# Masking the first batch on TensorE, and a new written order of the whole program

## The chip, the cores and the metric

The kernel runs on one core of one Trainium2 chip. The metric is the device time of one execution in microseconds (us); lower is better. The profile is that of one execution.

## The reference

Block-sparse attention is followed by a gated feed-forward block:

```
scores = (q @ k^T) / sqrt(64)                      # 4 batches, 8 heads, 768 tokens, 64 per head
scores = where(mask, scores, -1e9)                 # mask in blocks of 32 x 32 tokens: neighbours,
                                                   # first and last block, 3 sampled blocks a row
attn   = softmax(scores) @ v                       # -> x, 3072 tokens x 512
xn     = x / rms(x) * rms_g
out    = (silu(xn @ w_gate) * (xn @ w_val)) @ w_out   # 512 -> 1536 -> 512
```

The mask is the same for all batches and heads.

## The kernel before

**Tiling.** The 3072 tokens are twelve chunks of 256 (`ch` 0 to 11, three to a batch; `ic = ch % 3`). In a chunk attention goes over four pairs of heads (`pr`) and, in each pair, over three pieces of 256 keys (`j2`). One such piece is one score step `s0` to `s143`: `s12` to `s23` are chunk 1, `s24` to `s35` chunk 2, and so on. TensorE computes the transposed scores of two heads into two PSUM banks (L648), ScalarE takes the exponential of each bank (`x...`, L661), and after the three pieces TensorE multiplies by V (`av`, 24 matmuls, L678). V carries a column of ones, which gives the sum for the division (`on`, L690 and L692). Then come the squares (`sq`, L703 or L706), the power -1/2 on GpSimd (`rs`, L711), the scaling (`sc`, L717) and the transposition of x: on TensorE in chunks 0 and 1 (`xt`, L732, with the copies `xc`), by DMA from SyncE's queue later (`xd`).

The feed-forward part of a chunk `u` is six column pieces `g{u}_0` to `g{u}_5` of the two up projections (L835; 32 matmuls each), tanh (`th`, L842), two VectorE steps (`uu` L846, `h` L853), and the down projection `y{u}_t_part` (L868), whose result ScalarE copies out (`yo`).

**The mask** is applied in one of two ways. For the chunks that `PEM` names, TensorE adds a term to the scores in PSUM before the exponential. It comes from two small matrices, `KindG` and `NegQ`, and is 0 where a pair is allowed and -16384 where it is not (L653):

```python
def PEM(ch, pr):
    return ch == 0 or ch == 1 and pr < PM1        # PM1 = 0
...
start=True, stop=not PEM(ch, pr))
if PEM(ch, pr):
    nc.tensor.matmul(out=s_, lhsT=KindG[rows, 2 * j2 + jj, :],
        rhs=NegQ[rows, ic * CQ:(ic + 1) * CQ], start=False, stop=True)
```

All other chunks are multiplied after the exponential, on VectorE, by a mask of ones and zeros (`m{ch}_{pr}_{j2}`, L668). That mask, `Mk`, is made once, in nine tiles (`mt` on TensorE, `mk` on VectorE or ScalarE).

**Loads.** K, Q and V of batches 1 to 3 go through one staging buffer, `stage`. They are loaded in that order, each as two DMAs on GpSimd's queue (`l{b}_1_..` is K, `l{b}_0_..` Q, `l{b}_2_..` V), then cast: `c{b}_1_0` to `c{b}_1_5` for K, `c{b}_0_0` to `c{b}_0_5` for Q, `va{b}_0` to `va{b}_3` for V. The next of the three can load only when the last cast of the one before is done. The transposed K and Q of batches 1 to 3 come by DMA from SyncE's queue (`dt`). The weights use GpSimd's queue too: the up projections in six pieces (`wg`, `wv`), the down projection in two halves, `wo0_` and `wo1_` (L458). The parts 0 to 2 of `y0_0` need the first half, the parts 3 to 5 the second.

**Order.** The order of the instructions is written out: the string `ORDER` holds some 1500 steps, with the buffers (the digits after a colon) and, where two engines could do a step, the engine (`*DVE`, `*ACT`). Each engine executes its steps in this order, and each waits only for what it needs. The string was planned from assumed durations; the numbers in the `plan.add` calls are what such a planner uses, and at run time they do nothing. `FILL` sets the number of fillers `w0`, `w1`, ...: pairs of idle matmuls (L321).

GpSimd's steps from 40 us on are, in the string's order:

```
sta1_0 l1_0_0 l1_0_4 rs1 sta1_2 l1_2_0 wo1_ one1 l1_2_4 sta2_1 rs2 l2_1_0 l2_1_4
```

Of the kernel before, what the change touches and what calls it, by code (L numbers as in the profile page):

```python
# [27 lines left out]
x1_2_1_0 m1_0_1 sc0_0:0 sc0_1:1 e3_0_2*DVE w6:4 w7:4 xt0_0:10 xt0_1:4 s20:07 s21:36 x1_2_1_1 x1_2_2_0 x1_2_2_1
x1_3_0_0:3 xc0_0*DVE xc0_1*DVE m1_1_1 m1_1_2 m1_0_2 m1_2_1 m1_1_0 qk0 raw0 rawq1 xc0 w8:1 w9:2 g0_0a:12 g0_0
s22:45 s23:07 x1_3_0_1 th0_0:0 x1_3_1_0 x1_3_1_1 x1_3_2_0 x1_3_2_1 uu0_0:0 m1_2_2 h0_0:0 m1_3_0 m1_2_0  # L30
g0_1a:36 g0_1 s24:41 g0_2a:50 s25:72 g0_2 th0_1:1 x2_0_0_0:1 x2_0_0_1 x2_0_1_0 x2_0_1_1 th0_2:2 uu0_1:1 h0_1
m1_3_2 uu0_2:2 av1_0:4 s26:17 mt2_2:3 av1_2:2 s27:65 on1_0 m1_3_1 c1_1_0*DVE mk2_2*ACT x2_0_2_0 x2_0_2_1
x2_1_0_0:4 x2_1_0_1 c1_1_1*DVE c1_1_2*DVE c1_1_3*DVE c1_1_4*DVE c1_1_5*ACT h0_2 on1_2 g0_3a:31 s28:47 g0_3
av1_3:6 av1_1:5 w10:0 w11:0 s29:20 sta1_0 th0_3:0 x2_1_1_0 x2_1_1_1 x2_1_2_0 x2_1_2_1 on1_3 uu0_3:0 on1_1 h0_3
m2_0_2 m2_1_1 m2_1_2 sq1_0*ACT sq1_1*ACT l1_0_0 l1_0_4 rs1 s30:46 w12:7 g0_4a:37 g0_4 s31:25 s32:01 th0_4:1
x2_2_0_0:2 x2_2_0_1 x2_2_1_0 x2_2_1_1 x2_2_2_0 x2_2_2_1 uu0_4:1 sc1_0:2 sc1_1:3 h0_4 m2_0_1 m2_2_1 m2_2_0
m2_0_0 m2_2_2 c1_0_0*DVE c1_0_1*DVE c1_0_2*DVE c1_0_3*DVE w13:4 s33:43 w14:6 xt1_0:61 w15:2 xt1_1:5 s34:20
g0_5a:71 g0_5 xc1_0*ACT xc1_1*ACT x2_3_0_0:3 th0_5:2 x2_3_0_1 x2_3_1_0 x2_3_1_1 c1_0_4*ACT c1_0_5*ACT uu0_5:2
m2_3_1 h0_5 qk1 dt1_1_0 dt1_1_3 dt1_0_0 xc1 sta1_2 g1_0a:65 g1_0 g1_1a:43 g1_1 g1_2a:20 g1_2 s35:71 th1_0:0
th1_1:1 x2_3_2_0 x2_3_2_1 th1_2:2 uu1_0:0 uu1_1:1 m2_1_0 h1_0:1 h1_1 uu1_2:2 av2_2:6 mt0_0:4 s36:71 w16:5  # L40
s37:53 av2_0:2 mk0_0*ACT x3_0_0_0:0 x3_0_0_1 x3_0_1_0 x3_0_1_1 m2_3_0 h1_2 on2_0 on2_2 m2_3_2 l1_2_0 wo1_ one1
l1_2_4 s38:47 s39:15 s40:03 av2_1:2 av2_3:6 x3_0_2_0 x3_0_2_1 x3_1_0_0:2 x3_1_0_1 x3_1_1_0 x3_1_1_1 m3_0_1
on2_1 m3_1_0 on2_3 m3_0_2 m3_1_1 m3_0_0 va1_0*DVE va1_1*DVE va1_2*DVE va1_3*DVE s41:47 g1_3a:15 s42:20 s43:36
g1_3 x3_1_2_0 x3_1_2_1 x3_2_0_0:1 x3_2_0_1 x3_2_1_0 x3_2_1_1 th1_3:0 sq2_0 sq2_1 dt1_0_2 dt1_0_4 raw1 rawq2
sta2_1 rs2 l2_1_0 l2_1_4 y0_0_0:4 y0_0_1 s44:72 s45:03 y0_0_2 y0_0_3 y0_0_4 y0_0_5 av3_0:6 x3_2_2_0 x3_2_2_1
yo0_0:0 x3_3_0_0:4 x3_3_0_1 uu1_3:0 m3_1_2 h1_3 sc2_0:0 on3_0 m3_2_0 m3_2_2 m3_2_1 sc2_1:1 s46:17 s47:24
av3_1:5 s48:03 x3_3_1_0 x3_3_1_1 x3_3_2_0 x3_3_2_1 x4_0_0_0:3 x4_0_0_1 g1_4a:61 g1_4 s49:72 av3_2:4 s50:03
x4_0_1_0 th1_4:1 x4_0_1_1 x4_0_2_0 on3_1 m3_3_2 uu1_4:1 m3_3_1 on3_2 h1_4 m3_3_0 x4_0_2_1 g1_5a:57 g1_5 s51:26
s52:03 y0_1_0:4 y0_1_1 y0_1_2 av3_3:1 y0_1_3 th1_5:2 x4_1_0_0:0 x4_1_0_1 x4_1_1_0 c2_1_0*DVE c2_1_1*ACT
x4_1_1_1 c2_1_2*ACT uu1_5:2 on3_3 sq3_0 sq3_1 c2_1_3*DVE h1_5 c2_1_4*DVE c2_1_5*DVE m4_0_2 m4_0_1 xd2_0:2  # L50
xd2_1 qkfree0 xc2 qk2 dt2_1_0 dt2_1_3 sta2_0 l2_0_0 l2_0_4 rs3 y0_1_4 y0_1_5 s53:26 s54:05 g2_0a:31 g2_0
x4_1_2_0 x4_1_2_1 yo0_1:1 th2_0:0 x4_2_0_0:2 x4_2_0_1 uu2_0:0 h2_0:0 g2_1a:72 g2_1 s55:64 g2_2a:03 s56:51 g2_2
th2_1:1 x4_2_1_0 x4_2_1_1 x4_2_2_0 th2_2:2 x4_2_2_1 uu2_1:1 sc3_0:2 h2_1 sc3_1:3 m4_1_2 uu2_2:2 m4_0_0 h2_2
m4_1_1 m4_1_0 m4_2_0 m4_2_1 s57:67 y1_0_0:4 y1_0_1 y1_0_2 y1_0_3 y1_0_4 y1_0_5 s58:52 s59:10 x4_3_0_0:1
x4_3_0_1 yo1_0:2 x4_3_1_0 x4_3_1_1 x4_3_2_0 x4_3_2_1 g2_3a:67 g2_3 s60:43 g2_4a:52 s61:10 g2_4 th2_3:0
x5_0_0_0:4 x5_0_0_1 uu2_3:0 m4_2_2 m4_3_0 m4_3_1 x5_0_1_0 x5_0_1_1 th2_4:1 s62:46 av4_0:3 av4_2:1 av4_1:0
uu2_4:1 on4_0 on4_2 on4_1 m4_3_2 h2_3 h2_4 x5_0_2_0 c2_0_0*ACT x5_0_2_1 s63:45 g2_5a:36 g2_5 s64:10 av4_3:7
y1_1_0:2 y1_1_1 y1_1_2 y1_1_3 x5_1_0_0:3 c2_0_1*ACT c2_0_2*ACT c2_0_3*ACT th2_5:2 x5_1_0_1 on4_3 uu2_5:2
x5_1_1_0 h2_5 m5_0_0 c2_0_4*DVE c2_0_5*DVE x5_1_1_1 sq4_0 sq4_1 xd3_0:3 xd3_1 xc3 dt2_0_0 sta2_2 y1_1_4 y1_1_5
s65:45 g3_0a:71 s66:03 rs4 l2_2_0 l2_2_4 x5_1_2_0 x5_1_2_1 yo1_1:3 x5_2_0_0:2 x5_2_0_1 g3_0 s67:64 g3_1a:52  # L60
g3_1 s68:03 x5_2_1_0 x5_2_1_1 th3_0:0 th3_1:1 x5_2_2_0 x5_2_2_1 g3_2a:64 g3_2 s69:03 th3_2:2 x5_3_0_0:0
x5_3_0_1 va2_0*ACT m5_1_1 sc4_0:0 m5_1_0 uu3_0:0 uu3_1:1 h3_0:1 h3_1 m5_2_2 uu3_2:2 m5_0_2 g3_3a:75 g3_3
s70:12 y2_0_0:0 y2_0_1 y2_0_2 y2_0_3 y2_0_4 y2_0_5 s71:36 x5_3_1_0 th3_3:0 va2_1*ACT x5_3_1_1 va2_2*ACT
yo2_0:0 sc4_1:1 h3_2 m5_0_1 m5_3_1 uu3_3:0 m5_1_2 h3_3 x5_3_2_0 g3_4a:14 g3_4 s72:20 s73:73 y2_1_0:5 y2_1_1
y2_1_2 y2_1_3 x5_3_2_1 th3_4:1 x6_0_0_0:1 x6_0_0_1 uu3_4:1 h3_4 x6_0_1_0 x6_0_1_1 va2_3*ACT m5_2_1 m5_3_0
m5_2_0 m5_3_2 qkfree1 xd4_0:0 xd4_1 xc4 dt2_0_2 dt2_0_4 raw2 rawq3 sta3_1 y2_1_4 s74:62 s75:10 s76:74 av5_0:3
y2_1_5 x6_0_2_0 x6_0_2_1 yo2_1:1 x6_1_0_0:4 x6_1_0_1 x6_1_1_0 x6_1_1_1 av5_2:6 av5_3:2 av5_1:5 s77:10 on5_0
on5_2 m6_0_2 on5_3 on5_1 x6_1_2_0 x6_1_2_1 sq5_0 sq5_1 g3_5a:36 s78:72 g3_5 g4_0a:45 s79:10 g4_0 rs5 l3_1_0
l3_1_4 x6_2_0_0:2 x6_2_0_1 th3_5:2 x6_2_1_0 x6_2_1_1 th4_0:0 m6_1_2 m6_2_0 uu3_5:2 sc5_0:2 uu4_0:0 h4_0:0 h3_5
g4_1a:72 g4_1 g4_2a:13 g4_2 s80:04 th4_1:1 th4_2:2 x6_2_2_0 y3_0_0:5 y3_0_1 y3_0_2 y3_0_3 y3_0_4 y3_0_5 s81:60  # L70
x6_2_2_1 yo3_0:2 x6_3_0_0:0 x6_3_0_1 m6_2_1 uu4_1:1 uu4_2:0 h4_1 m6_2_2 sc5_1:3 h4_2 c3_1_0*DVE m6_1_1
c3_1_1*ACT g4_3a:74 g4_3 s82:12 s83:56 g4_4a:30 g4_4 th4_3:0 x6_3_1_0 m6_3_0 uu4_3:2 m6_1_0 c3_1_2*DVE h4_3
x6_3_1_1 x6_3_2_0 x6_3_2_1 g4_5a:17 g4_5 s84:25 s85:64 th4_4:1 c3_1_3*ACT uu4_4:1 m6_3_2 m6_0_1 c3_1_4*ACT
th4_5:2 x7_0_0_0:3 c3_1_5*ACT x7_0_0_1 x7_0_1_0 x7_0_1_1 uu4_5:0 h4_4 h4_5 m6_3_1 m6_0_0 xd5_0:1 xd5_1 xc5
sta3_0 y3_1_0:3 y3_1_1 y3_1_2 y3_1_3 y3_1_4 y3_1_5 s86:21 s87:50 s88:67 av6_2:4 yo3_1:3 x7_0_2_0 x7_0_2_1
# [88 lines left out]
def kernel(  # L164
# [20 lines left out]
    NP = H // 2  # L185
# [787 lines left out]
```

## Time and profile before

| | |
|---|---|
| median of six runs | 301.04 us (300.64 to 302.83) |
| the profiled execution | 300.78 us |
| its span on the core | 299.0 us |
| busy: PE, DVE, ACT | 286.1 us, 243.2 us, 232.2 us |
| VectorE mask multiplications (L668) | 132, 686 ns mean |
| TensorE mask matmuls (L653) | 48 |
| data moved by DMA | 39.76 MB |

PE is TensorE's matmuls, PEld its weight loads, DVE VectorE, ACT ScalarE, POOL GpSimd, SP SyncE. A row of the timeline is: start in us, length in us, engine, line, operation, what it writes and reads, how many instructions; in brackets, the idle time before it and what ended that. A row of a table of stretches is: from and to, length, then the busy us of PE, PEld, DVE, ACT and POOL with the count of instructions, the granted TensorE clock, the DMA share and GB/s. A row of loads ends with the KB of one and the us from issue to landing.

### The profile page before, as it was taken

What the parts mean: (1) busy time and instruction counts of PE and PEld (TensorE: products, weight loads), DVE (VectorE), ACT (ScalarE), POOL (GpSimd) and SP (SyncE); (2) the same over time, 40 slices, a digit from 0 to 9 for tenths busy, and PEclk for the clock granted to TensorE, in tenths of its full rate; (3) what the DMA queues carried; (4) which work ended last, traced back from release to release, by engine and by line L of the source; (5) the groups of instructions that cost most, each with busy time, mean ns of one, the idle gap of its engine ahead of it and who ended that gap; (6) DMA issues with size and microseconds to landing.
All of it is one profiled execution on the core that took longest, in us unless ns stands there. A gap on an engine that the chain in (4) does not pass through costs nothing.

```text
span 299.0 us, 10723 instructions
## 1 busy us (share of the span) xinstructions
PE 286.1 (96%) x4557; PEld 218.6 (73%) x4579; DVE 243.2 (81%) x501; ACT 232.2 (78%) x469; POOL 35.3 (12%) x56
## 2 busy tenths in 40 slices
PE   7999998995999999999999999999999999999995
PEld 4776987764776876787787678787778778678862
DVE  6679999985979979879988788999759889845840
ACT  7999989896698999978958899998398776242421
POOL 9531020303020030020100021000000000000000
PEclk9999999998899999999999999999999999999999
DMA  8999998993959944777543796502504104224003
GB/s 183 308 205 207 299 170 222 178 215 104 248 94 229 171 104 152 125 204 161 151 144 54 91 234 189 85 30 70 110 0 101 45 2 72 37 38 143 2 10 132
DMA packets 56692, 39.76 MB, mean 133 GB/s; under 512 B 42244, under 2 KB 50052, under 8 KB 56644
## 3 DMA queue, kind: packets, MB, share of 16 engines
q1 hardware_dynamic: 45268, 17.11, 31.6%
q0 software_dynamic: 10688, 21.50, 28.5%
q8 instruction: 36, 0.59, 0.8%
q10 hardware_dynamic: 688, 0.46, 0.5%
q14 instruction: 12, 0.10, 0.2%
HBM read 28.57 MB, written 6.29 MB: 117 GB/s over the span
## 4 chain that ended last, share of the span: by engine, by line
PE 81%; DVE 5%; DMA 5%; ACT 5%; issue 2%; POOL 1%; ACTq 0%
PE f L835 38%; PE f L868 20%; PE f L678 10%; PE f L648 9%; DMA stage<-in_v_dram 5%; ACT pt L661 4%; DVE pt L668 2%; PE f L321 2%; PE f L483 1%; DVE X L692 1%; DVE hp L853 1%; DVE uu L846 1%; PE f L732 1%; PE f L653 0%; ACT qb L269 0%
## 5 line engine op out<-in xcount | busy, mean ns | idle before, releaser
L661 ACT ACTIVATE pt<-f 128x512 bf16<-128x512 f32 x288 | 153.3, 639 | 11.7 <-PE f L648 11.4
L835 PE MATMUL f<-xn,wgv 64*128 64x256 bf16 x2304 | 137.5, 270 | 0.5 <-issue 0.5
L835 PEld LDWEIGHTS <-wgv 64*128 64x128 bf16 x2304 | 115.0, 94 | 13.3 <-issue 1.6
L668 DVE TENSOR_TENSOR pt<-pt,Mk 128x1024 bf16<-128x1024 bf16 x132 | 86.5, 686 | 4.2 <-ACT pt L661 4.1
L868 PE MATMUL f<-wo,hp 128*128 128x512 bf16 (+1 forms) x278 | 65.6, 370 | 2.8 <-DMA wo<-in_moe_w_out_dram 1.6
L842 ACT ACTIVATE th<-f 128x512 bf16<-128x512 f32 x72 | 44.0, 618 | 24.7 <-PE f L835 21.7
L846 DVE SCALAR_TENSOR_TENSOR uu<-th,f 128x512 bf16<-128x512 bf16 x72 | 48.7, 683 | 13.6 <-ACT th L842 13.5
L648 PE MATMUL f<-qkT 64*128 64x256 bf16 x576 | 52.9, 271 | 2.2 <-DVE uu L846 1.7
L853 DVE TENSOR_TENSOR hp<-uu,f 128x512 bf16<-128x512 bf16 x72 | 48.3, 684 | 2.2
L868 PEld LDWEIGHTS <-hp 128*128 128x128 bf16 x300 | 27.1, 98 | 31.3 <-issue 5.5
L678 PEld LDWEIGHTS <-pt 128*128 128x128 bf16 x1152 | 38.4, 97 | 8.0 <-issue 4.7
L678 PE MATMUL f<-va,pt 128*128 128x65 bf16 x1152 | 41.0, 194 | 0.9 <-DVE hp L853 0.6
L648 PEld LDWEIGHTS <-qkT 64*128 64x128 bf16 x576 | 26.4, 94 | 13.8 <-issue 10.1
L890 ACT ACTIVATE yo<-f 128x512 f32<-128x512 f32 (+1 forms) x24 | 14.1, 594 | 18.0 <-PE f L868 17.5
L711 POOL TENSOR_TENSOR rs<-ms,nhalf 128x2 f32<-128x2 f32 x12 | 9.1, 755 | 152.2 <-ACT junk L703 133.0
L717 DVE SCALAR_TENSOR_TENSOR x<-X,rs,gB 128x512 bf16<-128x512 f32 (+1 forms) x48 | 22.1, 514 | 3.4 <-POOL rs L711 3.4
L692 DVE TENSOR_TENSOR X<-f,rz 128x256 f32<-128x256 f32 x48 | 20.4, 425 | 1.7
L703 ACT ACTIVATE junk<-X 128x513 bf16<-128x513 f32 x22 | 14.1, 669 | 7.2 <-DVE X L692 7.2
L690 DVE RECIPROCAL rz<-f 128x4 f32<-128x4 f32 x48 | 8.5, 177 | 9.2 <-PE f L678 8.2
L321 PE MATMUL f<-idle 128*128 128x256 bf16 x48 | 8.8, 315 | 2.1 <-DVE idle L296 1.1
L275 POOL DMA_DIRECT2D stage<-in_q_dram x6 | 4.5, 762 | 41.8 <-ACT th L842 15.4
L269 DVE CAST va<-stage 128x768 bf16<-128x768 f32 x10 | 5.3, 554 | 4.5 <-DMA stage<-in_v_dram 4.4
(80 smaller groups left out, 111.4 us busy)
## 6 DMA issues: line engine op xcount, KB each, us to landing
stage<-in_v_dram POOLq DMA_DIRECT2D x8, 768.0 KB, 8.1
out_dram<-yo SPq DMA_DIRECT2D x23, 256.0 KB, 2.2
stage<-in_k_dram POOLq DMA_DIRECT2D x6, 768.0 KB, 7.0
stage<-in_q_dram POOLq DMA_DIRECT2D x6, 768.0 KB, 6.8
wgv<-in_moe_w_gate_dram POOLq DMA_DIRECT2D x3, 512.0 KB, 17.5
wgv<-in_moe_w_val_dram POOLq DMA_DIRECT2D x3, 512.0 KB, 19.3
wo<-in_moe_w_out_dram POOLq DMA_DIRECT2D x2, 768.0 KB, 17.2
xn<-x SPq DMA_TRANSPOSE x40, 3.6
```

Source lines behind the costliest of these rows:

```text
L321: nc.tensor.matmul(out=warm[:, 0:256], lhsT=idle[:, 0:P], rhs=idle, start=True, stop=True)
L648: nc.tensor.matmul(out=s_, lhsT=x[rows, 1, 2 * j2 + jj, pr, :], rhs=x[rows, 0, 2 * ic:2 * ic + 2, pr, :], start=True, stop=not PEM(ch, pr))
L661: nc.scalar.activation(out=pts[ch, pr][:, j2, e], in_=st[t][e], func=AF.Exp, scale=SCALE)
L668: nc.vector.tensor_tensor(out=pv, in0=pv, in1=m.unsqueeze(1).to_broadcast([P, 2, 2 * CQ]), op=ALU.mult)
L678: nc.tensor.matmul(out=o_[:, qt, e, 0:D + 1], lhsT=pt[:, jt // 2, e, jt % 2 * CQ + qt * P:jt % 2 * CQ + (qt + 1) * P], rhs=va[(ch // NIC) ...
L692: nc.vector.tensor_tensor(out=x1s[ch][:, :, 2 * pr * D:(2 * pr + 2) * D].rearrange("p t (h d) -> p t h d", h=2), in0=o4[:, :, :, 0:D], in1 ...
L717: nc.vector.scalar_tensor_tensor(out=x2[:, lo:lo + n], in0=x1s[ch][:, qt, 0:n], scalar=mss[ch][:, qt:qt + 1], in1=gB[:, 0:n], op0=ALU.mult ...
L835: nc.tensor.matmul(out=gst[u, fp, name][:, half * CQ:(half + 1) * CQ], lhsT=wgv[rows, dpart(i, c), f * P:(f + 1) * P], rhs=xns[u][rows, c, :],
L842: nc.scalar.activation(out=ths[u, fp], in_=gst[u, fp, "gp"], func=AF.Tanh, scale=0.5)
L846: nc.vector.scalar_tensor_tensor(out=uus[u, fp], in0=ths.pop((u, fp)), scalar=1.0, in1=gst.pop((u, fp, "gp")), op0=ALU.add, op1=ALU.mult)
L853: nc.vector.tensor_tensor(out=hps[u][:, 2 * fp:2 * fp + 2, :].rearrange("p f t -> p (f t)"), in0=uus.pop((u, fp)), in1=gst.pop((u, fp, "vp ...
L868: nc.tensor.matmul(out=yst[u, t, half][:, 0:n], lhsT=hps[u][:, f, t * P:(t + 1) * P], rhs=wo[:, f, cols], start=(f == 0), stop=(f == NF - 1))
```

## The change

1. `PEM` now names the first twelve pairs: all of chunks 0, 1 and 2, which is batch 0. Chunks 1 and 2 get the added matmuls and lose their 24 multiplications `m1_...` and `m2_...`.
2. Eleven fillers in place of 17.
3. Numbers of the planner: some landing and DMA times are set longer.
4. The string `ORDER` is planned anew. Names that stay move, change buffers, and 33 steps change between VectorE and ScalarE.

```diff
-    PM1 = 0
+    PMASK = 12
 
     def PEM(ch, pr):
-        return ch == 0 or ch == 1 and pr < PM1
-
-    FILL = 17
+        return ch * NP + pr < PMASK
+
+    FILL = 11
...
-    swdge("V4", lambda: load_v0(4), 2.4, [">V0"], -9, issue=0.75, extra=2.1)
+    swdge("V4", lambda: load_v0(4), 2.4, [">V0"], -9, issue=0.75, extra=2.8)
...
-                swdge(f"l{b}_{i}_{lo}", lambda b=b, i=i, lo=lo: load_part(b, i, lo, lo + 4), (3.6, 2.5, 2.5)[i],
+                swdge(f"l{b}_{i}_{lo}", lambda b=b, i=i, lo=lo: load_part(b, i, lo, lo + 4), 2.6,
...
-                     deps=[f"qk{b}"] + ([">" + prev] if prev else []) + [f"c{b}_{i}_{c}" for c in range(c0, c1)], dma=0.7 * (c1 - c0), prio=1)
+                     deps=[f"qk{b}"] + ([">" + prev] if prev else []) + [f"c{b}_{i}_{c}" for c in range(c0, c1)], dma=1.2 * (c1 - c0), prio=1)
```

On GpSimd's queue the new order is

```
sta1_0 l1_0_0 l1_0_4 rs1 sta1_2 l1_2_0 l1_2_4 wo1_ one1 sta2_1 l2_1_0 l2_1_4 rs2
```

so the second half of the down projection, which was issued between the two halves of batch 1's V, is issued behind both. Earlier on the same queue `rs0` now stands ahead of batch 1's K (`rs0 l1_1_0 l1_1_4 wo0_`, before `l1_1_0 l1_1_4 wo0_ rs0`).

The steps of ScalarE around batch 1's Q (the casts `c1_0_...`) are now

```
x2_2_2_1 th0_4 c1_0_0 x2_3_0_0 th0_5 xc1_0 x2_3_0_1 x2_3_1_0 x2_3_1_1 c1_0_5 x2_3_2_0 th1_0
```

and were

```
x2_2_2_1 xc1_0 xc1_1 x2_3_0_0 th0_5 x2_3_0_1 x2_3_1_0 x2_3_1_1 c1_0_4 c1_0_5 th1_0
```

TensorE's steps from the second chunk's feed-forward part on are now

```
w7 w8 s35 g1_0 g1_1 g1_2 av2_1 s36 s37 av2_0 mt0_0 s38 av2_3 s39 s40 av2_2 s41 g1_3a s42 g1_3
s43 s44 w9 w10 s45 y0_0_0 y0_0_1 y0_0_2 y0_0_3 y0_0_4 y0_0_5 s46 s47 s48 av3_0 av3_1 g1_4
```

and were

```
g1_0 g1_1 g1_2 s35 av2_2 mt0_0 s36 w16 s37 av2_0 s38 s39 s40 av2_1 av2_3 s41 g1_3a s42 s43 g1_3
y0_0_0 y0_0_1 s44 s45 y0_0_2 y0_0_3 y0_0_4 y0_0_5 av3_0 s46 s47 av3_1 s48 g1_4
```

## The prediction

> **What bounds the kernel now.** I read the page first.
>
> ```profile
> span 299.0 us, 10723 instructions
> PE 286.1 (96%) x4557; PEld 218.6 (73%) x4579; DVE 243.2 (81%) x501; ACT 232.2 (78%) x469; POOL 35.3 (12%) x56
> ...
> PE   7999998995999999999999999999999999999995
> ...
> DVE  6679999985979979879988788999759889845840
> ...
> PEclk9999999998899999999999999999999999999999
> ```
>
> TensorE is busy nearly everywhere. The exceptions are the start, the end, and slices 9 to 11 (60 to 82 us), where the granted clock dips too. Next I cut the span into stages, from 28.9 us, where the feed-forward matmuls begin.
>
> ```profile
> 28.90:66.20 37.30, 36.15 (x647) 29.81 (x648) 36.84 (x76) 34.47 (x70) 4.87 (x7) 1.00 1.04 216
> 66.20:81.00 14.80, 10.88 (x170) 8.38 (x172) 9.80 (x22) 9.63 (x22) 2.26 (x3) 0.88 0.80 184
> 81.00:264.00 183.00, 181.38 (x2911) 137.41 (x2928) 158.02 (x309) 150.39 (x307) 14.38 (x19) 1.00 0.51 109
> ```
>
> After 81 us PE is busy 181.38 of 183 us and the view of waits has 0.7 us of waits for it: that part is TensorE's own work, which the change leaves alone, so a VectorE relief is worth nothing there. From 28.9 to 66.2 us VectorE is full (36.84 of 37.30) with PE close behind. The hole is 66 to 81 us. The timeline of PE:
>
> ```profile
> 66.13 0.61 PE L868 MATMUL f<-wo,hp 128*128 128x512 bf16 x2
> 68.33 1.46 PE L868 MATMUL f<-wo,hp 128*128 128x512 bf16 x6 [1.59 <-DMA wo<-in_moe_w_out_dram]
> 69.62 0.89 PE L678 MATMUL f<-va,pt 128*128 128x65 bf16 x24
> 72.25 0.61 PE L648 MATMUL f<-qkT 64*128 64x256 bf16 x8 [1.74 <-DVE uu L846]
> 73.45 1.48 PE L678 MATMUL f<-va,pt 128*128 128x65 bf16 x24 [0.59 <-DVE hp L853]
> 74.86 0.61 PE L648 MATMUL f<-qkT 64*128 64x256 bf16 x4
> ```
>
> First y0_0_3 waits for wo1. Then s46 waits for a bank that uu1_3 frees. Then av3_1 takes 1.48 us where av3_0 took 0.89: the clock is at half from 73.07 to 76.48 us (granted 0.50 there). VectorE tells why uu1_3 is late:
>
> ```profile
> 65.10 1.02 DVE L269 CAST va<-stage 128x768 bf16<-128x768 f32 x2
> 70.57 1.03 DVE L269 CAST va<-stage 128x768 bf16<-128x768 f32 x2 [4.45 <-DMA stage<-in_v_dram]
> 71.52 0.68 DVE L846 SCALAR_TENSOR_TENSOR uu<-th,f 128x512 bf16<-128x512 bf16 x1
> ```
>
> It stands at va1_2 for the second half of batch 1's V. GpSimd's issues, and the rows of the two late loads:
>
> ```profile
> 53.88 0.79 POOL L275 DMA_DIRECT2D stage<-in_v_dram  x1 [8.38 <-ACT qb L269]
> 54.67 0.84 POOL L458 DMA_DIRECT2D wo<-in_moe_w_out_dram  x1
> ...
> 55.61 0.77 POOL L275 DMA_DIRECT2D stage<-in_v_dram  x1
> ```
>
> ```profile
> wo<-in_moe_w_out_dram POOLq DMA_DIRECT2D x1, 768.0 KB, 13.6
> stage<-in_v_dram POOLq DMA_DIRECT2D x1, 768.0 KB, 14.9
> ```
>
> V's first half has 7.6 us to landing. So the three land at 61.5, 68.3 and 70.55 us, in the order of issue: wo1 takes 6.8 us behind V, and V's second half 2.3 us behind wo1.
>
> **Masks.** The change removes 24 multiplications of VectorE. In a run of five they take 3.09 us, 0.605 each, so 14.5 us. It adds 24 x 4 = 96 matmuls. Their price stands in the timeline of chunk 0:
>
> ```profile
> 9.87 0.29 PE L648 MATMUL f<-qkT 64*128 64x256 bf16 x2
> 9.99 0.28 PE L653 MATMUL f<-NegQ,KindG 64*128 64x256 bf16 x2
> ```
>
> A pair starts 0.11 us after the pair before, so 0.055 us a matmul and 5.2 us in all. Here the Trainium skill speaks against the change: the page "TensorE: Matmul & The Clock Gate", section "Back-to-back issue gap", gives N/2.4 + 2.5 ns for one, 109 ns at 256 columns, which makes 10.5 us. The row shows 109 ns for two, since the two heads use different halves of the array's rows; I take 5.2. Twelve filler matmuls go, 0.109 us each (eight take 1.09): -1.3. So TensorE has 3.9 us more to do, all of it before 57 us.
>
> **What covers it.** From 6.4 us to the wait for wo1, adding up the matmuls (L835, L648 and the like 0.055, L868 0.217, L678 0.0305) leaves about 11 us in which PE does fillers or nothing, half before 28.9 us, where ScalarE runs without a gap. I walked the new order through with these durations. ScalarE's 24 exponentials of chunk 0 now have e2_0_0, e3_0_0, va0_2 and mk0_1 among them (about 1.9 us), and start 0.5 us sooner, as kc0 and e0_0_0 went to VectorE: the first feed-forward matmul moves from 28.9 to about 30.5 us. g1_0 moves from 50.2 to about 52.2. From there to y0_0_3 TensorE has 96 matmuls (5.25), four av (2.9), ten unmasked score steps (2.2), g1_3 (1.75), y0_0_0 to 2 (1.3) and the rest (0.6): 14 us, plus about 2 us of waits for exponentials. It arrives at y0_0_3 at about 68.2 us, before at 66.7. That is off the path as long as wo1 lands later.
>
> **The loads.** V is issued when Q's last cast is done. ScalarE now does c1_0_0 when Q lands (50.0 us before; K ahead of it is bound by the weights' queue and not by its issue, so rs0 ahead of K costs nothing unless it is over 5 us late), then x2_3_0_0, th0_5, xc1_0, three exponentials and c1_0_5: 0.5 x 5 + 1.0 + 0.5 = 4.0 us. V goes out at about 54.2 us, 0.3 later. Its first half lands at about 61.8, the second 2.3 behind at 64.1. va1_2 then waits for nothing, and uu1_3 and h1_3, queued behind it, free their banks in time. wo1 now lands behind both: 68.3 + 2.3 + 0.3 = 70.9 us. y0_0_3 stalls from 68.2 to 70.9, and s46, s47, s48, av3_0 and av3_1 are queued behind it. rs2 is now behind batch 2's K on GpSimd, which waits for va1_3; both are done before sq2_1, so this costs nothing. If va1_3 were late again, sc2 and xd2 would be late with it.
>
> **The sum**, from wo1's landing to g1_4a. Before: 75.26 - 68.28 = 6.98 us. Work in it: y 1.30, av3_0 and av3_1 1.46, three score steps 0.65, so 3.4. Lost: 3.6, and half of the 1.2 us of half clock still to come, 0.6: 4.2. After: only the work, but 2.6 us later. Gain 1.6 us on the profiled 300.78; the same off the median, which lies 0.26 above it: 301.04 - 1.6 = **299.4 us**. After 81 us I take no change; the redrawn order there could cost up to 1 us, and can gain hardly anything.
>
> **Rivals.**
> *(a) The stall is kept short and the clock stays whole:* the sum above, 299.4; own range 298.6 to 300.2.
> *(b) The half clock comes anyway.* The skill's same page, section "HAM oscillation", warns of idle gaps above about 3.4 us; by it a stall of 2.7 us is free, and (a) holds. The trace disagrees: no gap reached 2 us, yet 1.46 busy us in 3.41 (69.66 to 73.07) brought half clock, while 1.82 (66.25 to 69.66) did not. A stall of 2.7 us leaves little over 0.7 busy us if it lies in one such stretch, and passes if it straddles two. Price 3.41 / 2 = 1.7: 301.1.
> *(c) wo1 lands about when PE arrives.* A K load issued at 130 us, without transposes beside it, landed after 5.0 us and not 7.6. If V's first half does that, everything is 2.6 us earlier: 4.2 us gained, 296.9. Against: Q's transposes go out at the same time as before.
> *(d) Slower: Q lands late.* c1_0_0 now stands ahead of th0_5 and xc1_0 on ScalarE, so a late Q holds g1_0, V and wo1, each us for a us. The price passes the gain at 1.6 us and gives over 0.5% from 3.2 us: 303. Against: K's casts, which release Q's load, come off a VectorE that is freed. The same sum would follow from any late c1_0_5.
> *(e) It does otherwise than its title says.* "Ahead of V" would take the wait from PE and leave VectorE's. The order puts wo1 behind both halves of V, and I go by the order.
>
> **How the numbers follow.** (a) 0.42, (b) 0.22, (c) 0.23, (d) 0.13. 0.5%, about what a measurement of this kernel can tell from no change, is 1.5 us: 299.5 to 302.5. (a) lies at that bound and gives 0.29 to faster and 0.13 to same; (c) is faster; (b) is same; (d) is slower. Faster 0.52, same 0.35, slower 0.13. The range reaches (c) and (b) with a little of (d): 296.7 to 302.4.
>
> **What would show it.** Right: 36 score steps with L653 and 108 multiplications; VectorE waits under 1 us at va1_2; PE's longest wait after 30 us is at L868 for wo, 2 to 3.5 us, ending at 70 to 72 us; g1_4a at about 74.3. Wrong: that wait is gone (c), PEclk at half behind it (b), ScalarE waits for Q's landing and g1_0 starts after 54 (d), or PE has waits above 1 us after 81 us, which would mean that the new order fails where I assumed nothing.

## The result: 0.6% faster, and the profile after

| | before | after |
|---|---|---|
| median | 302.20 us (299.91 to 304.50) | 300.81 us (297.73 to 304.62) |
| ratio | | 0.9939, interval 0.9920 to 0.9959 |
| the profiled execution, its span | 300.78 us, 299.0 us | 300.91 us, 299.1 us |
| first feed-forward matmul (g0_0), g1_0, g1_4 | 28.9, 50.2, 75.3 us | 31.8, 54.6, 76.6 us |
| wo1 lands | 68.3 us | 72.9 us |

The kernel before was run again beside the new one, which is why its median differs from the one the prediction started from. 0.9939 of 302.2 is 1.8 us less; the prediction said 1.6. Each ratio here leaves out executions far above the fastest of their own kernel: of the new kernel these are 11 of 34, nine of them with the half clock treated further below, and with them the medians alone differ by 1.4 us (0.9955).

The two profiled executions took the same time, because that of before was a quick one (1.4 us under its median) and that of after a typical one. So they show what changed inside, and not the gain. The page of after, to be read against that of before:

```profile
span 299.1 us, 10875 instructions
PE 287.3 (96%) x4639; PEld 220.8 (74%) x4663; DVE 234.6 (78%) x484; ACT 229.0 (77%) x462; POOL 36.3 (12%) x56
...
PE   8979999996999999999999999999999999999995
...
DVE  5628587787989969989979999789988998845740
...
PEclk9999999999999999999999999999999999999999
```

VectorE is busy 8.6 us less and TensorE 1.2 us more. (VectorE's mask multiplications alone fell by 16.1 us, from 86.5 to 70.4; other steps came to it.) The granted clock stays whole; the dip of slices 10 and 11 is gone. The same stages as before:

```profile
28.90:66.20 37.30, 36.81 (x703) 32.55 (x702) 27.90 (x63) 31.33 (x62) 6.04 (x9) 1.00 0.98 212
66.20:81.00 14.80, 11.70 (x180) 8.39 (x179) 12.19 (x25) 12.57 (x28) 2.67 (x3) 1.00 0.99 207
81.00:264.00 183.00, 181.90 (x2938) 137.88 (x2957) 161.84 (x316) 149.54 (x306) 15.27 (x19) 1.00 0.49 110
```

In the first stage VectorE was full before (36.84 us) and is idle a quarter of the time now (27.90); TensorE went from 36.15 to 36.81. The DMA share was about full in that stage and still is (1.04, 0.98): VectorE's relief did not make the loads shorter. In the hole, 66 to 81 us, TensorE is busy 0.8 us longer. TensorE's timeline has this, with one wait, at 20.59 us, that the profile of before does not have:

```profile
20.59 0.64 PE L481 MATMUL f<-ident,qb 128*64 128x128 bf16 x16 [1.34 <-DMA qb<-in_q_dram]
...
69.48 0.39 PE L646 MATMUL f<-qkT 64*128 64x256 bf16 x4 [1.11 <-ACT pt L659]
69.80 1.47 PE L866 MATMUL f<-wo,hp 128*128 128x512 bf16 x5
72.92 1.46 PE L866 MATMUL f<-wo,hp 128*128 128x512 bf16 x6 [1.65 <-DMA wo<-in_moe_w_out_dram]
74.31 0.83 PE L646 MATMUL f<-qkT 64*128 64x256 bf16 x12
75.07 1.63 PE L676 MATMUL f<-va,pt 128*128 128x65 bf16 x48
76.63 1.59 PE L833 MATMUL f<-xn,wgv 64*128 64x256 bf16 x26
```

After the wait for wo1 (1.65 us) nothing is late: s46 to s48 start without the 1.74 us wait, av3_0 and av3_1 take 1.63 us together at full clock. VectorE still waits for V's second half, but not as long (before 4.45 us), and the bank that s46 needs is free in time:

```profile
65.69 0.55 DVE L267 CAST va<-stage 128x768 bf16<-128x768 f32 x1
66.16 0.68 DVE L666 TENSOR_TENSOR pt<-pt,Mk 128x1024 bf16<-128x1024 bf16 x1
69.28 1.03 DVE L267 CAST va<-stage 128x768 bf16<-128x768 f32 x2 [2.43 <-DMA stage<-in_v_dram]
```

GpSimd's queue:

```profile
56.87 1.54 POOL L273 DMA_DIRECT2D stage<-in_v_dram  x2 [10.19 <-ACT qb L267]
58.40 0.84 POOL L456 DMA_DIRECT2D wo<-in_moe_w_out_dram  x1
```

V goes out at 56.9 us, 3 us later than in the profile of before. Its halves land at 62.8 and 69.3 us, and wo1 at 72.9. One reason for the late issue stands on ScalarE, which waits for batch 1's Q:

```profile
52.09 0.62 ACT L267 CAST qb<-stage 128x512 bf16<-128x512 f32 x1 [1.37 <-DMA stage<-in_q_dram]
```

### The profile page after: what moved, and what is told of

The parts are those of the page before. It is cut to its first block, busy times and chain, and to the rows that moved or that the text cites. A ratio compares the mean times of both kernels' runs of the same rounds, so it can differ in the third digit from the quotient of the medians.

```text
span 299.1 us, 10875 instructions
## 1 busy us (share of the span) xinstructions
PE 287.3 (96%) x4639; PEld 220.8 (74%) x4663; DVE 234.6 (78%) x484; ACT 229.0 (77%) x462; POOL 36.3 (12%) x56
## 4 chain that ended last, share of the span: by engine, by line
PE 81%; DMA 9%; DVE 4%; ACT 3%; POOL 2%; issue 1%; POOLq 0%; ACTq 0%; DVEq 0%
PE f L833 39%; PE f L866 20%; PE f L676 10%; PE f L646 9%; DMA qb<-in_q_dram 5%; DMA stage<-in_v_dram 4%; ACT pt L659 2%; DVE pt L666 2%; PE f L651 1%; POOL stage L273 1%; DVE x L715 1%; POOL kb L262 0%; PE f L730 0%; ACT xn L267 0%; POOL qb L258 0%
## 5 line engine op out<-in xcount | busy, mean ns | idle before, releaser
L833 PE MATMUL f<-xn,wgv 64*128 64x256 bf16 x2304 | 135.7, 269 | 0.5 <-DVE X L690 0.3
L833 PEld LDWEIGHTS <-wgv 64*128 64x128 bf16 x2304 | 113.6, 94 | 13.5 <-issue 1.3
L666 DVE TENSOR_TENSOR pt<-pt,Mk 128x1024 bf16<-128x1024 bf16 x108 | 70.4, 686 | 0.8 <-ACT pt L659 0.5
L646 PE MATMUL f<-qkT 64*128 64x256 bf16 x576 | 55.1, 270 | 1.7 <-ACT pt L659 1.3
L646 PEld LDWEIGHTS <-qkT 64*128 64x128 bf16 x576 | 27.9, 94 | 11.1 <-issue 6.7
L709 POOL TENSOR_TENSOR rs<-ms,nhalf 128x2 f32<-128x2 f32 x12 | 10.3, 856 | 137.8 <-ACT junk L701 109.7
L701 ACT ACTIVATE junk<-X 128x513 bf16<-128x513 f32 x20 | 13.1, 659 | 8.2 <-DVE X L690 8.1
L651 PE MATMUL f<-NegQ,KindG 64*128 64x256 bf16 x144 | 18.4, 269 | 0.0
L651 PEld LDWEIGHTS <-KindG 64*128 64x128 bf16 x144 | 8.6, 94 | 2.0 <-issue 1.4
L273 POOL DMA_DIRECT2D stage<-in_v_dram x8 | 6.1, 772 | 26.4 <-DVE X L690 16.0
```

What stands on the lines that cost most here:

```text
L646: nc.tensor.matmul(out=s_, lhsT=x[rows, 1, 2 * j2 + jj, pr, :], rhs=x[rows, 0, 2 * ic:2 * ic + 2, pr, :], start=True, stop=not PEM(ch, pr))
L651: nc.tensor.matmul(out=s_, lhsT=KindG[rows, 2 * j2 + jj, :], rhs=NegQ[rows, ic * CQ:(ic + 1) * CQ], start=False, stop=True)
L666: nc.vector.tensor_tensor(out=pv, in0=pv, in1=m.unsqueeze(1).to_broadcast([P, 2, 2 * CQ]), op=ALU.mult)
L833: nc.tensor.matmul(out=gst[u, fp, name][:, half * CQ:(half + 1) * CQ], lhsT=wgv[rows, dpart(i, c), f * P:(f + 1) * P], rhs=xns[u][rows, c, :],
```

## The experiments

Each ratio is to the kernel before, run on the same chip; 0.5% is 1.5 us. The diffs show the steps of the written order, or the lines of code, that differ.

### The masks alone, the loads alone

The first takes the order of before, lets TensorE mask all of batch 0 and drops the 24 multiplications from the order. The second takes the kernel before and moves one load.

```diff
 # masks alone, in the kernel before
-        return ch == 0 or ch == 1 and pr < PM1
+        return ch * NP + pr < PMASK        # PMASK = 12
 # and without the steps m1_0_0 ... m2_3_2 of the order

 # loads alone, in the kernel before
-l1_2_0 wo1_ one1 l1_2_4
+l1_2_0 one1 l1_2_4 wo1_
```

> Kernel before, with batch 0 masked on TensorE and the 24 multiplications dropped from the order; nothing else moves, wo1 stays between V's halves. Theory (the loads set the end of the stage up to 75 us): VectorE is relieved but still waits for V's second half at about 70.5 us, and TensorE has 5.2 us more; ratio to before 0.998 to 1.008. Rival (VectorE's relief is the gain): ratio 0.990 to 0.995.

> Kernel before, with wo1 issued behind V's second half; masks as before. Theory: V's second half lands about 6 us sooner, wo1 about 2.3 us later (70.6); one wait of about 4 us at y0_0_3 takes the place of three waits of 4 us in all, and half clock follows it; gain 0 to 1.9 us, ratio 0.994 to 1.000. Rival (VectorE's relief is the gain): 1.000 to 1.008, since the wait at TensorE only grows.

Measured: masks alone 304.23 us, ratio 1.0074 (1.0036 to 1.0112); loads alone 300.38 us, ratio 0.9951 (0.9928 to 0.9974). The load order by itself gives about all of the gain, and the masks by themselves make the kernel slower. VectorE and TensorE of the masks alone:

```profile
76.47 1.03 DVE L267 CAST va<-stage 128x768 bf16<-128x768 f32 x2 [4.18 <-DMA stage<-in_v_dram]
...
78.14 0.92 PE L646 MATMUL f<-qkT 64*128 64x256 bf16 x8 [2.74 <-DVE uu L844]
```

These are the two waits of the kernel before (4.45 and 1.74 us), each 6 us later, most of which is that V goes out at 59.1 us and not at 53.9. V is late because Q is: Q's second half, issued at 44.2 us (before 41.6), took 12.9 us to land (before 8.4). Why it took longer stays open. VectorE's free time is worth nothing while it ends in the same wait. With the loads alone both are gone, and what is left is TensorE's own wait for wo1:

```profile
66.74 1.96 DVE L269 CAST va<-stage 128x768 bf16<-128x768 f32 x4
...
71.80 1.46 PE L868 MATMUL f<-wo,hp 128*128 128x512 bf16 x6 [3.42 <-DMA wo<-in_moe_w_out_dram]
```

VectorE takes V's four casts in a row. The wait for wo1 is 3.42 us, more than any wait of TensorE in this stretch before, and the kernel is still faster: one long wait is cheaper here than a shorter one with VectorE's wait behind it. From V's issue to g1_4 it takes 20.0 us (55.53 to 75.52), where the kernel before took 21.4 (53.88 to 75.26).

### wo1 back between the halves of V, in the new kernel

```diff
-l1_2_0 l1_2_4 wo1_ one1
+l1_2_0 wo1_ l1_2_4 one1
```

> Changed kernel, with wo1 issued between V's halves again. Theory: TensorE's wait for wo1 (1.65 us) goes, VectorE waits for V's second half until about 73 us, and uu1_3 comes only after two casts and four multiplications (4 us), so score step 46 starts near 77 us in place of 74.3: 2 to 3 us slower than the changed kernel, ratio to before 1.000 to 1.005. Rival (masks are the gain, the load order is nothing): ratio as the changed kernel, 0.994.

Measured: 305.30 us, ratio 1.0110 (1.0068 to 1.0153). That is more than was expected: against the new kernel 1.7% (1.0110 - 0.9939), 5 us, three times what the same load is worth in the old order. The old waits return, 2 and 4 us later than they were:

```profile
72.32 1.03 DVE L267 CAST va<-stage 128x768 bf16<-128x768 f32 x2 [3.68 <-DMA stage<-in_v_dram]
...
76.41 0.39 PE L646 MATMUL f<-qkT 64*128 64x256 bf16 x4 [2.29 <-DVE uu L844]
```

Not all of the 5 us is theirs: g1_4 starts at 79.4 us, 2.7 us later than in the new kernel, and all six of these executions had the half clock at least once. The new kernel's own executions with half clock have medians of 303.4 and 303.6 us, under 2 us below this run's 305.3. So the place of this load is probably worth less than 5 us, and how they divide stays open.

### wo1 far ahead, with the masks on either engine

If the wait for wo1 bounds the new kernel, issuing it right behind Q should take the wait away. The same edit was made in the new kernel, in the kernel before, and in the kernel before with the masks on TensorE.

```diff
 # new kernel
-l1_0_0 l1_0_4 rs1 ... l1_2_0 l1_2_4 wo1_ one1
+l1_0_0 l1_0_4 wo1_ rs1 ... l1_2_0 l1_2_4 one1
 # kernel before (and with PMASK = 12 and no m1_, m2_ steps)
-l1_0_0 l1_0_4 rs1 ... l1_2_0 wo1_ one1 l1_2_4
+l1_0_0 l1_0_4 wo1_ rs1 ... l1_2_0 one1 l1_2_4
```

> Changed kernel, with wo1 issued right behind batch 1's Q, so ahead of both halves of V. Theory: wo1 lands near 59 us, in time that the queue of these loads has idle (52 to 57 us); no wait at y0_0_3, V at most 2 us later; no half clock. Gain over the changed kernel 1.5 to 3 us, ratio to before 0.984 to 0.990. Rival (TensorE's own work with the added masks sets the time): as the changed kernel, 0.994.

> Kernel before, old masks, with wo1 issued right behind batch 1's Q, so ahead of both halves of V. Theory (the loads hold the stage up to 75 us, not VectorE): wo1 lands near 59 us and V near 62 and 65, so neither y0_0_3 nor va1_2 waits; g1_4a near 71 in place of 75.3 and no half clock: gain 3 to 5.5 us, ratio 0.982 to 0.990. Rival (VectorE's masks fill the stage anyway, 98% busy): gain under 1 us, ratio 0.997 to 1.000.

> The same as the run with wo1 ahead of V and old masks, but batch 0 masked on TensorE (the 24 multiplications dropped). Theory: with no wait for loads left, TensorE's own work counts; it has 5.2 us more, of which part fills gaps: 1 to 4 us slower than that run, ratio to before 0.988 to 1.000. Rival (VectorE full is the bound of the stage): 1 to 3 us faster than that run.

Measured: in the new kernel 301.76 us, ratio 0.9960 (0.9928 to 0.9992); in the kernel before 300.24 us, 0.9923 (0.9894 to 0.9952); there with the masks on TensorE 302.12 us, 0.9991 (0.9960 to 1.0021).

The new kernel gains nothing from it, as the rival had it. Its profile has no wait for wo1 any more, but wo1 now loads beside Q; the profiled execution also had 6.8 us of half clock from 21 us on, so its marks cannot be set against those of the new kernel. The kernel before gains, but less than its marks promise and than the theory said: g1_4 starts at 72.6 us, 2.7 us earlier, and g2_0 at 86.9, 1.8 us later. In this profile, which is of one of its slowest executions (303.30 us, median 300.24), the next load in the chain is why:

```profile
85.00 0.43 DVE L269 CAST kb<-stage 128x512 bf16<-128x512 f32 x1 [5.70 <-issue]
...
84.19 1.94 PE L868 MATMUL f<-wo,hp 128*128 128x512 bf16 x5 [3.64 <-issue]
...
70.97 1.54 POOL L275 DMA_DIRECT2D stage<-in_k_dram  x2
```

VectorE stands at the cast of batch 2's K. The trace names no releaser ("issue"), but the second half of K landed at 84.92 us, just before. It had been issued at 71.8 and took 13.2 us; the four DMA transposes of x, issued from 71.8 to 77.6 us, took 9.5 to 13.1 us beside it. Whether this load is as late in the quicker executions is not shown.

Masks on TensorE against masks on VectorE, all else equal: 0.9991 - 0.9923 = 0.7%, and in the first pair 1.0074 against 1 = 0.7%. Twice about 2.1 us, for 5.2 us of matmuls. The stretch from g0_0 to g1_0, in which 52 of the 96 matmuls lie (52 x 0.055 = 2.9 us), shows the price most plainly. It takes 21.3 us in all four profiles with the old order and the masks on VectorE (before, loads alone, wo1 behind Q, and the version that beats both), and 23.25 us in both profiles with the masks on TensorE: 1.9 us more. In both of these Q also takes 13 us to land, so some of the 2.1 us may come by way of V's late issue.

### x's copies ahead of Q's cast on ScalarE

The prediction's rival (d) put Q's cast, ahead of th0_5 and xc1_0, down as a risk. This is the new kernel with wo1 behind Q and the two first casts moved behind those.

```diff
-h0_4 c1_0_0*ACT g0_5a ... s34:52 c1_0_1*DVE x2_3_0_0:1 th0_5:2 xc1_0*ACT xc1_1*DVE uu0_5:2
+h0_4 g0_5a ... s34:52 x2_3_0_0:1 th0_5:2 xc1_0*ACT xc1_1*DVE c1_0_0*ACT c1_0_1*DVE uu0_5:2
```

> Changed kernel with wo1 issued right behind batch 1's Q, and the casts c1_0_0 and c1_0_1 of Q moved behind the two copies xc1, so that a late Q no longer holds the second chunk's feed-forward part. Theory (the wait for Q holds g1_0 in the changed kernel): g1_0 1 to 2 us sooner, total 1 to 2 us below the changed kernel with wo1 first (0.996), ratio to before 0.988 to 0.993. Rival (Q's landing doesn't matter there): 0.994 to 0.997.

Measured: 299.91 us, ratio 0.9934 (0.9911 to 0.9956). Against the same kernel without it (0.9960, 0.9928 to 0.9992) that may be 0.3%, but the intervals overlap. So the cost of this step is not decided.

### The new kernel once more

> The changed kernel unaltered, for a second profile and on the same chip as the others: ratio 0.992 to 0.996. In the profile the wait for wo1 at y0_0_3 is 1.5 to 4 us, and PE before 30 us waits for the last piece of batch 0's Q (1.3 us in the first profile) again if that piece lands after 19 us.

Measured: 301.15 us, ratio 0.9950 (0.9925 to 0.9976). A second profile of it shows how far two executions of one kernel lie apart: g0_0 at 30.5 us (31.8 in the first), g1_0 at 53.7 (54.6), g1_4 at 75.9 (76.6), wo1 at 72.2 (72.9). The last of the up-projection weights lands at 34.2 us here, at 35.6 there, and from 33.8 to 37.2 us over all profiles of this study. So a mark of one profile is good to 1 us at best. The kernel before shows more: loads alone, wo1 behind Q and the version that beats both are the same program as before up to g0_0, which starts at 28.9, 30.6, 31.1 and 31.4 us in these four profiles. The length of a stretch repeats better than its marks do: the 21.3 us from g0_0 to g1_0 agree to 0.02 us in the same four.

The wait at 20 us is not in this profile, and the wait for wo1 is longer (2.38 us, in the first profile 1.65):

```profile
19.27 0.64 PE L481 MATMUL f<-ident,qb 128*64 128x128 bf16 x16
...
72.21 1.46 PE L866 MATMUL f<-wo,hp 128*128 128x512 bf16 x6 [2.38 <-DMA wo<-in_moe_w_out_dram]
```

### The masks back on VectorE, in the new order

```diff
-    PMASK = 12
+    PMASK = 4
 # and 24 steps back in the order, each behind ScalarE's next step, like
-s16:13 x1_0_2_0 x1_0_2_1
+s16:13 x1_0_2_0 m1_0_1 x1_0_2_1
```

> Changed kernel with chunks 1 and 2 masked on VectorE again: the 24 multiplications stand in the new order, each behind the second exponential after its own pair, and the 96 matmuls are gone. Theory (the masks on TensorE cost 2 us, the loads and the new order bring the gain): VectorE, which waits 2 to 3 us for tanh and loads between 34 and 60 us in the changed kernel, takes them in; ratio to before 0.986 to 0.994. Rival (the new order needs VectorE free): VectorE becomes late for the casts of Q and V; ratio 0.996 to 1.006.

Measured: 317.53 us, ratio 1.0527 (1.0489 to 1.0565), far worse than either expectation. TensorE starves from 29 us on:

```profile
28.90:66.20 37.30, 26.77 (x405) 21.71 (x405) 31.30 (x63) 22.80 (x45) 5.62 (x7) 0.86 0.68 149
```

26.77 us busy, where the new kernel has 36.81. A likely reason, argued and not traced: VectorE's list is in an order, and a multiplication that waits for its exponentials holds the copies, the casts and the releases behind it. Q goes out at 51.6 us (42.4 in the new kernel), V at 69.7, and wo1 lands at 87.3. The new order is not good for masks on VectorE where they were put here. So the masks' share of the gain can't be had by subtraction: 0.7% is their price in the old order; in the new order no price of theirs could be had this way.

### Work for TensorE at the first wait

The new kernel's wait at 20.59 us is for the last piece of batch 0's Q. Here av0_2 goes ahead of the transposes that wait.

```diff
-s11:10 t0_0_2:7 x0_3_1_0 ... x0_3_2_1 on0_0 e0_0_2*DVE ... qk0 t1_0_2:5 av0_2:4 s12:67
+s11:10 x0_3_1_0 ... x0_3_2_1 av0_2:4 t0_0_2:7 on0_0 e0_0_2*DVE ... qk0 t1_0_2:5 s12:67
```

> Changed kernel with av0_2 ahead of the two transpositions that wait for the last piece of batch 0's Q. Theory (that wait, 1.3 us at 19 us, costs its length, and brings half clock in the third of executions in which it is longest): 0.7 us of work goes into the wait, and executions with half clock fall from about 3 in 10 to 1 in 10 or less; median 0.7 to 1.5 us below the changed kernel, ratio to before 0.989 to 0.993. Rival (the start is hidden behind the loads): as the changed kernel, 0.994 to 0.995.

Measured: 300.43 us, ratio 0.9952 (0.9928 to 0.9976): as the rival had it, the median is not below the new kernel's. What changed is the half clock. How often a kernel met the half clock can be read from each execution's mean granted clock (one stretch of 3.4 us lowers it from 1.000 to about 0.994):

| | none | one stretch | two |
|---|---|---|---|
| before (141, in four sets) | 23 | 75 | 43 |
| new kernel (34 and 22) | 40 | 16 | 0 |
| av0_2 first (19) | 19 | 0 | 0 |

With the new kernel's rate of 16 in 56, 19 in a row without one would come up 2 times in 1000. This speaks for the wait at 20 us as what brings the half clock into the new kernel. It is no proof: the profile of this run also waits only 0.25 us for wo1, where the new kernel's two wait 1.65 and 2.38, and no profile of the new kernel caught a half clock. In the new kernel it is dear: medians of 303.4 and 303.6 us with it, 300.2 and 300.7 without. In the kernel before one stretch costs next to nothing: in its four sets of runs the median with one is 0.2 us under to 0.6 us over that without; with two it is 0.9 to 1.8 us over. Over all executions the new kernel's medians are 0.9955 and 0.9974 of those of before, that of av0_2 first is 0.9963, and that of the loads alone 0.9932, so of these the smallest edit has the lowest ratio.

### A version that beats both

The kernel before, with its masks on VectorE, wo1 behind Q, V's casts drawn ahead of three multiplications, and batch 2's K issued as soon as they are done, and so ahead of the transposes of x.

```diff
-on2_3 m3_0_2 m3_1_1 m3_0_0 va1_0*DVE va1_1*DVE va1_2*DVE va1_3*DVE s41:47 ... sta2_1 rs2 l2_1_0 l2_1_4
+on2_3 va1_0*DVE va1_1*DVE va1_2*DVE va1_3*DVE sta2_1 l2_1_0 l2_1_4 m3_0_2 m3_1_1 m3_0_0 s41:47 ... rs2
```

> Kernel before, old masks, wo1 issued behind Q (0.992 alone), and the casts of V moved ahead of three masks, with batch 2's K issued ahead of rs2 and directly behind them. Theory (the gain of wo1 first was given back at 79 us, where VectorE waited 5.7 us for batch 2's K, late since its load ran beside four transpositions of x): K goes out 2 to 3 us sooner and lands before 78 us; that wait falls under 2 us; 1 to 3 us faster than with wo1 first alone, ratio to before 0.982 to 0.989. Rival (the loads' bandwidth is the bound up to 85 us, whatever their order): 0.991 to 0.994.

Measured: 297.27 us, ratio 0.9873 (0.9827 to 0.9919), just below the interval of the changed kernel (from 0.9920), and below that of the loads alone (from 0.9928). The interval of wo1 behind Q alone (0.9894 to 0.9952) overlaps it, so what K's place adds by itself is likely but not decided by six executions. The half clock is not gone from it: three of the six executions had one stretch, one had two. That last one, the slowest (301.77 us), is the one profiled; its half clock lies at 8.2 and 100.4 us, away from the hole. The hole is closed:

```profile
68.61 1.90 PE L868 MATMUL f<-wo,hp 128*128 128x512 bf16 x8
70.35 0.89 PE L678 MATMUL f<-va,pt 128*128 128x65 bf16 x24
71.18 0.75 PE L648 MATMUL f<-qkT 64*128 64x256 bf16 x8
71.86 0.90 PE L678 MATMUL f<-va,pt 128*128 128x65 bf16 x24
72.69 0.39 PE L648 MATMUL f<-qkT 64*128 64x256 bf16 x4
72.92 2.00 PE L835 MATMUL f<-xn,wgv 64*128 64x256 bf16 x32
...
68.03 1.49 POOL L275 DMA_DIRECT2D stage<-in_k_dram  x2 [9.98 <-DVE va L269]
```

No row of this stretch of TensorE has a wait. K, issued 2.9 us earlier than with wo1 behind Q alone, lands at 72.9 and 75.0 us, and no cast waits for it. g2_0 starts at 82.3 us, where it was 85.1 before, though V went out 2.5 us later here (56.4 us, before 53.9).

### Each mask matmul of chunks 1 and 2 twice

The disputed cost by itself: the new kernel with 96 more mask matmuls, nothing moved. The mask is added twice, so the output is the same.

```diff
-                if PEM(ch, pr):
+                for k in range(2 if ch in (1, 2) else PEM(ch, pr)):
```

> The changed kernel with every mask matmul of chunks 1 and 2 of batch 0 issued twice (the mask is added twice, so the result is the same): 96 more matmuls of 0.055 us, 5.2 us of TensorE, and nothing else changed. Theory, that TensorE has next to no idle time between 30 and 55 us in the changed kernel, where chunk 1 and part of chunk 2 lie, so that the mask matmuls are covered there only in part: 2.5 to 4 us slower than the changed kernel, a ratio to the kernel before of 1.002 to 1.008; g1_0 moves 2 to 3 us later and with it the issue of V's load and the landing of wo1. Rival, the prediction's step, that the loads set the end of this stage and TensorE's gaps take up the masks: wo1 lands when it did, g1_4 stays near 76, and the ratio is 0.994 to 0.998.

Measured: 302.24 us, ratio 1.0002 (0.9978 to 1.0027), 0.5 to 0.6% above the new kernel's two ratios, so 1.6 to 1.9 us for 5.2 us of matmuls. That is under what the theory gave and above what the rival gave. The price of one is plain in the timeline, where four mask matmuls (29.50) hold the next scores up for 0.22 us (29.72), so 0.055 each:

```profile
29.39 0.29 PE L646 MATMUL f<-qkT 64*128 64x256 bf16 x2
29.50 0.39 PE L651 MATMUL f<-NegQ,KindG 64*128 64x256 bf16 x4
29.72 0.28 PE L646 MATMUL f<-qkT 64*128 64x256 bf16 x2
29.83 0.39 PE L651 MATMUL f<-NegQ,KindG 64*128 64x256 bf16 x4
...
72.02 2.76 PE L867 MATMUL f<-wo,hp 128*128 128x512 bf16 x12 [0.65 <-ACT pt L660]
```

The table of stretches has the first stage:

```profile
28.90:66.20 37.30, 37.20 (x708) 33.42 (x708) 24.89 (x54) 28.07 (x54) 4.84 (x8) 1.00 0.98 202
```

The measured time has a part of each. TensorE is busy 37.20 of 37.30 us: the gaps are used up, and g1_0 starts at 57.3 us, 2.7 to 3.6 us later than in the new kernel's two profiles, as the theory said. The stretch from g0_0 to g1_0, with 52 more mask matmuls in it, takes 25.3 us, 2.1 to 2.5 more than in those two. But wo1 lands only 0.4 to 1.1 us later (73.3 us), the 12 matmuls of the down projection, starting at 72.0, then run without a wait for it, and g1_4 starts at 77.2, 0.6 to 1.3 us later. The new kernel's wait for wo1 took up the rest, as the rival said.

## Why the prediction was right, and which of its steps were not

**The bound, and the end.** Right. After 81 us TensorE is busy 181.90 of 183 us (before 181.38), with no wait that the view of waits lists in the first profile and one of 1.0 us in the second, and VectorE's 8.6 us of relief are worth nothing there. In the old order they are worth nothing before 81 us either (masks alone, 1.0074).

**The load order makes the gain.** Right, and shown: alone it gives 0.9951, taken back it gives 1.0110 (with more half clock, as said). The chain that the prediction read (V's second half, va1_2, uu1_3, s46) is the one that goes. From V's issue to g1_4 the prediction had 20.1 us (54.2 to 74.3); measured are 19.8 and 20.0, loads alone 20.0, before 21.4. From wo1's landing to g1_4 it had 3.4; measured are 3.75 in both profiles, before 6.98. Rival (e) falls: wo1 goes behind V, as the order says, and V's second half does not wait for it.

**The sum.** 1.8 us by the ratio against 1.6 predicted, but the terms of the sum moved against each other:

| term | predicted | after, two profiles |
|---|---|---|
| g0_0; g1_0 | 30.5; 52.2 | 31.8, 30.5; 54.6, 53.7 |
| from g0_0 to g1_0 (before 21.3) | 21.7 | 22.8, 23.2 |
| V goes out | 54.2 | 56.9, 55.9 |
| V's halves land | 61.8, 64.1 | 62.8 and 69.3; 61.6 and 68.6 |
| wo1 lands | 70.9 | 72.9, 72.2 |
| TensorE reaches y0_0_3 | 68.2 | 71.3, 69.8 |
| stall there | 2.7 | 1.65, 2.38 |
| g1_4 | 74.3 | 76.6, 75.9 |

Most of it is 1 to 3 us late (V's second half 5), and g1_4, which was to start 1.0 us sooner than in the profile of before, starts 0.7 to 1.4 us later. The prediction took one execution, 0.26 us under a median of six, for typical. The median of 70, 1.4 us above it, shows it was not, and so does the profile of the loads alone: it is the kernel before up to V's issue, and has g0_0 at 30.6, g1_0 at 51.9 and V at 55.5, each 1.6 us later than the profile of before. Set against those, the new kernel's V goes out 0.4 to 1.3 us later. It saves 1.4 to 1.6 us from V to g1_4, so 0.3 to 1.0 us of gain is left at g1_4. Where the rest of the measured 1.8 comes from is not shown, and that it is so near to the predicted 1.6 is in part luck.

**"What covers it": the step that failed.** The prediction spread 11 us of gaps (counted again with its durations, nearer 13) over 60 us, and the masks lie in part of it. From 30 to 60 us, with those durations, matmuls and fillers leave TensorE 4.5 us before and 2.1 after; the fillers are 1.5 and 0.9 more. For the stretch from g0_0 to g1_0 the prediction added 0.4 us to before's 21.3, where the two profiles have 1.5 and 1.9 more, and the masks alone 1.9. Over the whole kernel the masks cost about 2.1 us in the old order (twice), and doubling them 1.6 to 1.9 us, of 5.2. So there is cover for some 3 us of them. Part of it is the wait for wo1, which the prediction had named. That g0_0 is 1.3 us later in the first profile than in the second is not the masks' doing: the first has the wait of 1.34 us for Q at 20 us, the second does not.

**The price of a mask matmul.** The prediction took the row, 0.055 us, over the estimate of 10.5 us for all 96 that follows from the Trainium skill's page "TensorE: Matmul & The Clock Gate", section "Back-to-back issue gap". The row was right: in the doubled kernel four mask matmuls take 0.22 us, 0.055 each.

**The loads' landings.** The load of V to wo1 took 16.0 and 16.3 us from the first issue, predicted 16.7. Inside that, V's second half came 6.5 and 6.9 us behind the first, predicted 2.3 from the one case in the trace. So VectorE still waits 2.43 and 2.71 us, where the prediction's sign of being right was under 1 us. V's issue was late by 2.7 and 1.7 us. Most of that is Q, which landed at 52.1 and 51.1 us and not at 50.0; the rest is the way from there to V's issue, 4.8 us in both profiles and 4.2 in the prediction, whose sum of ScalarE's steps left out the first cast itself (about 0.5).

**The rivals.** *(c)* no: V's first half took 5.9 us, less than 7.6, but wo1 was no earlier. *(d)* came in part: ScalarE did wait for Q, 1.37 us in the first profile and 1.63 in the second, and g1_0 passed the 54 us of its sign in the first (54.6). The argument against it, that Q's load would go out sooner, did not hold: Q was issued at 42.4 and 41.2 us, before at 40.8. The kernel was not slower all the same, and the experiment on it decides nothing. *(b)* came in another form: half clock, in 16 of 56 executions, and most likely not from the stall at wo1. The likely source is the wait at 20 us for the last piece of batch 0's Q. The prediction walked through ScalarE's start of the program and not through the transposes' inputs: in the new order TensorE can reach them before Q has landed. The section "HAM oscillation" of the same page warns of gaps above about 3.4 us. The wait at this place is 1.34 us in the new kernel's first profile, at whole clock. It is 1.87 and 2.05 us in two relatives (wo1 between V's halves, and wo1 behind Q in the new kernel), whose clock is at half from 21.0 us on, in the second of them while the wait still lasts:

```profile
22.41 1.06 PE L481 MATMUL f<-ident,qb 128*64 128x128 bf16 x16 [2.05 <-DMA qb<-in_q_dram]
```

So half clock came here with gaps far under 3.4 us, and the measurement decides. The length of a wait is no sure sign the other way either: loads alone waited 3.42 us for wo1 and the new kernel's second profile 2.38, both at whole clock.

## What to carry to other kernels

Where loads share one queue and one staging buffer, look first at which load each engine stands at, and give each engine the load it reaches first; moving one word of the order was worth as much as planning the program anew. When a wait has been removed, check the next load of the chain: it may be issued into heavier traffic than before, and then the gain is given back 10 us on. Count the slack that is to cover added work in the stretch where that work lies, and not over the whole stage. Between profiles, compare the lengths of stretches before the times of marks: an execution that starts 2 us late shifts every mark.

## What the runs showed of the hardware

- **DMA transposes issued right beside a load went with a longer load.** The two halves of batch 2's K took 8.1 and 13.2 us when issued at 71.0 us with four DMA transposes beside them, and 4.9 and 6.2 us when issued at 68.0, ahead of them. The transposes gained as well: 9.5 to 13.1 us in the first case, 2.7 to 5.5 in the second. All fourteen profiles agree: in the two in which the first transpose of x went out within 0.9 us of K's first half, K's second half took 9.2 and 13.2 us; in the twelve with 2.2 us or more between them it took 6.2 to 7.8.
- **V's second half** came 2.2 to 2.5 us behind the first in six of the profiles in which it goes out next to it (among them loads alone, av0_2 first, masks twice) and 6.5 to 6.9 us in both of the new kernel. Q's transposes run beside V in all of them. What makes the difference was not found.
- **The half clock's price depends on its place.** 3.41 us at half speed cost 1.7 us of matmul time at most; in the kernel before, whose profile has it behind the wait for wo1, one stretch changed the median by -0.2 to +0.6 us; in the new kernel, by about 3 us. The latter is more than the clock itself can cost, so something else must be later in those executions too, perhaps the wait that brings it; two profiles of relatives of that kernel suggest it (1.87 and 2.05 us against 1.34), and no profile of the new kernel itself has caught one.
